# The fourth expert job in split form, its weights fetched early into staging buffers: a gated scan with a mixture of experts on Trainium2

## The chip, the cores and the metric

The kernel runs on one core of one Trainium2 chip. The metric is the device time of one execution in microseconds (us). An execution is repeated, and the median is quoted; one further execution is recorded by the hardware profiler.

## What is computed

The reference first runs a gated linear recurrence over 4 sequences of 3648 tokens with 256 features, and then sends every token to one of 16 experts.

```python
f = lower_bound + (1 - lower_bound) * sigmoid(f_logit)
for t in range(S):                       # per sequence
    h = f[:, t] * h + (1 - f[:, t]) * x[:, t]
    y[:, t] = h
# y is taken as 14592 rows of 256
g = argmax(y @ w_group)                  # one of 4 groups
e = argmax(y @ w_expert[g])              # one of 4 experts in it
out = softmax weights of g and e * (relu(y @ w1[g, e]) @ w2[g, e])   # 256 -> 1024 -> 256
```

All numbers are float32.

## The kernel before

**Units and jobs.** The tokens are cut into 29 units of 512 (28 full and one half). For each unit, phase 1 makes the gate, scans, writes the rows back in row form, computes the router's logits, and scatters each row to its expert's list in device memory. Of a group of units (one unit each for the first eight, then two) the routing is done together. The experts' work is cut into jobs. A job "A" takes the first rows of one expert's list as soon as enough units are scattered (its cut, the first number in `EARLY`); there are 16, and the first four take 256 rows each with cuts at units 4, 6, 8 and 8. A job "B" takes the rest of a list once all is scattered. Jobs are numbered from 0 here, as in the code: the fourth job is job 3.

**Two forms of a job.** A job with `j.raw` (line 865) multiplies in float32: its weights go by DMA straight into the weight tiles (line 959), `raw1` (line 1063, the matmuls at line 1071) makes the hidden layer, and `raw2` (line 1106, matmuls at line 1110) the output. ScalarE alone evicts the hidden layer (line 1074). A job in split form takes each float32 value as the sum of a float16 high part and a bfloat16 low part. Its weights land in a staging buffer `st` (line 963); `job_split` casts them on ScalarE (line 971) and subtracts on VectorE (line 973), four pieces to a job. The rows are cast at line 1042 and their low part is a subtraction at line 1043, with a small copy of the rows' numbers at line 1048. The first layer is three matmuls for each float32 one (lines 1097 to 1099), evicted by ScalarE (line 1102) and VectorE (line 1103) together; the second layer is line 1129.

**The order.** The main loop goes over the jobs. While it writes out job n it also writes out the preparation of job n+1 (`prep_thunks`: four times fetch and split, then the rows) and pieces of phase 1, paced by `due` marks. A raw job's second layer stands directly behind its first; that of a split job is left pending and stands behind the first layer of the next job. On SP (the queue that issues the loads) the written order is the executed one. On the other engines a planner of the framework reorders the main loop's instructions by its estimates.

**Fetching.** All weight pieces stand in one list, four to a job. `fetch_to(n)` issues loads until piece n; a job must have been chosen (`picked`) first. Job 0's pieces are fetched on its choosing, those of jobs 1 and 2 right behind job 0's row load (line 721). After that each preparation step fetches at most two pieces more, up to four ahead for a raw job and eight ahead for a split one (line 1215). There are 8 staging buffers, which units 4 to 7 of phase 1 use first for their inputs, and 3 buffers for each of the four weight tiles.

Of the kernel before, what the change touches and what calls it, by code (L numbers as in the profile page):

```python
# [22 lines left out]
EARLY = [(4, 2), (6, 2), (8, 2), (8, 2), (10, 2), (10, 2), (12, 3), (14, 3),  # L23
         (16, 4), (18, 4), (20, 4), (22, 5), (24, 5), (26, 5), (28, 5), (28, 5)]
# [8 lines left out]
ROWS_AT = {4: 5, 6: 7}  # L33
USED = float(1 << 22)
STG_BUFS = 8
RAW = 4
BOOK = 10
XR_BUFS = 6
ROW_BUFS = 6
# [14 lines left out]
def gated_scan_moe(ctx: ExitStack, tc, zx, lower, wroute, wexp, out, S):  # L54
# [391 lines left out]
    def p1_thunks(us, groups, parts):  # L446
# [54 lines left out]
        for u in us + [us[-1] + 1]:  # L501
            seq = []
            if u <= FAST:
# [39 lines left out]
                for m in [m for m, v in ROWS_AT.items() if u == v]:  # L543
                    f = lambda m=m: early_rows(m)
                    f.mark = m
                    put(f)
# [11 lines left out]
                if u == FAST:  # L558
                    f = lambda: None
                    f.mark = "begun"  # L560
                    put(f)
                    for v in [v for v in sorted(cuts) if v <= FAST and v not in ROWS_AT]:
                        f = lambda v=v: early_rows(v)
                        f.mark = v
                        put(f)
# [31 lines left out]
            if u - 1 in ends:  # L597
                grp = ends[u - 1]
                T = sum(unit_range(v)[1] - unit_range(v)[0] for v in grp) // P
                G = {}  # L600

                def bind(G=G, first=grp[0]):
                    G.update(cur.pop("G"))
                    G["rows"] = group_rows.pop(first)
                if u <= 13:
                    s1, f4x, s2, f3, f4, s6, f5, s7s = route_thunks(G, T, True)
                    rs = [s1, s2, f3, f4x, None, f4, s6, f5]
                else:
                    s1, s2, s3, s4, s5, s6, s7s = route_thunks(G, T)
                    rs = [s1, s2, s3, None, None, s4, s5, s6]  # L610
                rs.append(("scat", s7s))
                put(bind)
                rs.append(lambda u=u: choose(u))
                if u in cuts:
                    rs.append(lambda u=u: place(u))
                    f = lambda u=u: early_rows(u)
                    f.mark = u
                    rs.append(("lag", f))
                hold.extend(rs)
# [68 lines left out]
    def blanks():  # L688
        while unblanked:
            j = unblanked.pop(0)  # L690
            m = 1 if EARLY[j.idx][1] == 2 else 2
            sync.dma_start(out=xs_v[NT + j.idx][bass.ds(j.e * LW + (PRE - m * P), m * P), :].rearrange("(p k) c -> p k c", k=m),
                           in_=blank[:, None, :].broadcast_to([P, m, RW]))
# [20 lines left out]
    def early_rows(u):  # L714
        for mac in macros:
            for j in mac:
                if j.kind == "A" and EARLY[j.idx][0] == u and j.idx < NE - 1:
                    job_rows(j)
        ready[0] = True
        if u == EARLY[0][0]:  # L720
            fetch_to(pptr[0] + 8)

    regs = {}
    early_loads = []
# [115 lines left out]
    def make_job(kind, idx):  # L840
# [6 lines left out]
        while at < j.len:  # L847
# [16 lines left out]
            at += w  # L864
        j.raw = kind == "A" and idx < RAW
        j.wh, j.wl, j.st = {}, {}, {}
# [88 lines left out]
    def job_weights(j, i):  # L955
        e = job_e(j)
        if j.raw:
            w = wp.tile([P, 1024], F32, name=f"w{i}")
            sync.dma_start(out=w, in_=wexp[bass.ds(e * P, P), i * 1024:(i + 1) * 1024])
            j.wh[i], j.wl[i] = w[:, 0:512], w[:, 512:1024]  # L960
            return
        st = stg.tile([P, 1024], F32, name="st")
        sync.dma_start(out=st, in_=wexp[bass.ds(e * P, P), i * 1024:(i + 1) * 1024])
        j.st[i] = st
# [199 lines left out]
    pptr = [0]  # L1164
# [24 lines left out]
    def bg_to(n):  # L1189
        while done[0] < n:  # L1190
            bg_pop()

    def fetch_to(n):
        while pptr[0] < min(n, len(pieces)):
            j, i = pieces[pptr[0]]
            if j.kind == "A" and j.idx not in picked:
                return
            if j.kind != "A":
                bg_to(marks["order"])
            job_weights(j, i)  # L1200
            pptr[0] += 1
        if ready[0]:
            ready[0] = False
            blanks()
# [158 lines left out]
```

## Time and profile before

| | us |
|---|---|
| median of 3 runs | 761.43 |
| the three runs | 761.33, 761.43, 763.17 |
| the profiled execution | 761.96 |
| its span in the trace | 760.2 |
| TensorE (PE) busy in the span | 715.6 |
| VectorE (DVE) busy | 514.6 |
| ScalarE (ACT) busy | 445.9 |
| GpSimd (POOL) busy | 296.3 |

The trace records each instruction with its start, its duration, and the releaser of the idle time before it. PE's matmuls are pipelined, so the distance between the starts of neighbours is what one costs, and not the recorded duration of one. "PEld" is the loading of weights into PE. A view by stretches adds up the busy time of every engine between two times, and what is missing from the stretch is waiting.

### The profile page before, as it was taken

How to read it: one execution, taken by the hardware profiler on the slowest of the kernel's cores; microseconds unless marked ns; L12 is line 12 of the kernel's file. 1: busy time of each engine (PE TensorE's matmuls, PEld its weight loads, DVE VectorE, ACT ScalarE, POOL GpSimd, SP SyncE). 2: the span in 40 equal slices, each digit the busy share in tenths (PEclk: the TensorE clock that was granted, in tenths of full speed). 3: DMA queues.
4: the chain of work that ended last, by engine and by line, in shares of the span. 5: the costliest groups of instructions: out<-in, count | busy, mean ns of one | idle time of the engine just before them, and what ended most of it. 6: DMA issues, size and time to landing. Idle time of an engine off the chain costs nothing.

```text
span 760.2 us, 17863 instructions
## 1 busy us (share of the span) xinstructions
PE 715.6 (94%) x6471; PEld 588.0 (77%) x6471; DVE 514.6 (68%) x1086; ACT 445.9 (59%) x827; POOL 296.3 (39%) x314
## 2 busy tenths in 40 slices
PE   3569999998899999999999999999999999999995
PEld 1457888886788888888999676867778886777895
DVE  6899758999799976495556754644644645755660
ACT  6567767887577855454545644544544545655651
POOL 3656267668567764632222121312122121123232
PEclk9999999999999999999999999999999999999998
DMA  8978789989888873657994470617155345655520
GB/s 326 413 255 292 243 351 289 408 316 310 289 258 292 242 211 117 170 146 189 222 241 106 113 189 29 169 43 188 47 155 131 114 133 168 196 174 170 168 65 23
DMA packets 100410, 151.35 MB, mean 199 GB/s; under 512 B 60203, under 2 KB 70206, under 8 KB 97504
## 3 DMA queue, kind: packets, MB, share of 16 engines
q1 hardware_dynamic: 85792, 102.84, 46.1%
q0 software_dynamic: 11408, 30.02, 10.7%
q10 hardware_dynamic: 3120, 17.34, 6.7%
q8 instruction: 51, 0.84, 0.5%
q14 instruction: 39, 0.32, 0.1%
HBM read 112.49 MB, written 37.96 MB: 198 GB/s over the span
## 4 chain that ended last, share of the span: by engine, by line
PE 71%; DVE 11%; issue 8%; DMA 3%; POOL 3%; ACT 2%; another core or an unknown queue 1%; SPq 1%; POOLq 0%; DVEq 0%
PE ps_m L1129 28%; PE ps_m L1099 7%; PE ps_m L1097 7%; PE ps_m L1098 7%; PE ps_m L1110 4%; PE ps_m L1071 4%; PE ps_p L1097 3%; PE ps_p L1098 3%; PE ps_p L1099 3%; PE ps_p L284 3%; POOL out_dram L1143 3%; DVE h L256 2%; DVE w L973 1%; PE ps_p L303 1%; DVE hl L1103 1%
## 5 line engine op out<-in xcount | busy, mean ns | idle before, releaser
L1129 PE MATMUL ps_m<-w,hh 128*128 128x256 f16 (+5 forms) x1260 | 218.9, 268 | 1.3 <-issue 1.3
L1129 PE MATMUL ps_m<-w,hl 128*128 128x256 f16 (+4 forms) x740 | 188.5, 267 | 0.6 <-issue 0.6
L973 DVE TENSOR_TENSOR w<-st,w 128x1024 bf16<-128x1024 f32 x112 | 135.8, 1219 | 68.2 <-ACT w L971 66.7
L393 POOL DMA_INDIRECT xs<-rows,posi x114 | 138.2, 1212 | 87.6 <-ACT rows L288 25.6
L1143 POOL DMA_INDIRECT out_dram<-o,info x67 | 71.6, 1069 | 244.1 <-ACT o L1141 226.6
L1129 PE MATMUL ps_m<-w,rows 128*128 128x256 f16 (+5 forms) x880 | 133.8, 267 | 0.3 <-issue 0.3
L1129 PEld LDWEIGHTS <-hh 128*128 128x128 f16 (+7 forms) x1260 | 117.9, 101 | 15.6 <-issue 3.3
L971 ACT CAST w<-st 128x1024 f16<-128x1024 f32 x112 | 116.1, 1047 | 17.6 <-PE ps_m L1129 12.5
L1097 PE MATMUL ps_m<-xh,w 128*128 128x256 f16 (+9 forms) x494 | 120.4, 256 | 2.5 <-DVE hl L1103 2.4
L1099 PE MATMUL ps_m<-xh,w 128*128 128x256 f16 (+9 forms) x494 | 120.3, 256 | 0.8 <-issue 0.8
L1098 PE MATMUL ps_m<-xl,w 128*128 128x256 bf16 (+9 forms) x494 | 120.3, 256 | 0.0
L1103 DVE SCALAR_TENSOR_TENSOR hl<-ps_m,hh 128x512 bf16<-128x512 f32 (+7 forms) x107 | 71.1, 671 | 40.6 <-ACT hh L1102 24.7
L1098 PEld LDWEIGHTS <-w 128*128 128x128 f16 x800 | 78.3, 98 | 25.3 <-issue 3.7
L1097 PEld LDWEIGHTS <-w 128*128 128x128 f16 x800 | 78.3, 98 | 23.2 <-issue 1.6
L1099 PEld LDWEIGHTS <-w 128*128 128x128 bf16 x800 | 78.3, 98 | 22.8 <-issue 0.4
L1143 POOL DMA_INDIRECT out_dram<-o,meta x47 | 53.4, 1136 | 101.8 <-ACT o L1141 69.1
L1129 PEld LDWEIGHTS <-rows 128*128 128x128 f16 (+4 forms) x880 | 81.6, 101 | 10.0 <-issue 0.6
L1102 ACT ACTIVATE hh<-ps_m 128x512 f16<-128x512 f32 (+7 forms) x107 | 63.3, 594 | 37.1 <-PE ps_m L1099 32.1
L1141 ACT ACTIVATE o<-ps_m,info 128x256 f32<-128x256 f32 (+4 forms) x67 | 31.1, 463 | 91.5 <-PE ps_m L1129 75.8
L1129 PEld LDWEIGHTS <-hl 128*128 128x128 bf16 (+4 forms) x740 | 70.8, 101 | 9.1 <-issue 1.9
L256 DVE TENSOR_TENSOR_SCAN h<-zt,h 128x512 f32<-128x512 f32 (+3 forms) x48 | 56.6, 1191 | 0.5
L1103 DVE SCALAR_TENSOR_TENSOR hh<-ps_p,rows 128x512 bf16<-128x512 f32 (+7 forms) x30 | 17.6, 586 | 45.4 <-ACT rows L1102 45.3
(203 smaller groups left out, 1183.4 us busy)
## 6 DMA issues: line engine op xcount, KB each, us to landing
st<-in_wexp_dram SPq DMA_DIRECT2D x112, 512.0 KB
zt<-in_zx_dram ACTq DMA_DIRECT2D x16, 1024.0 KB
w<-in_wexp_dram SPq DMA_DIRECT2D x16, 512.0 KB
xs<-blank SPq DMA_DIRECT2D x26, 258.0 KB
zt<-in_zx_dram SPq DMA_DIRECT2D x6, 1024.0 KB
st<-in_zx_dram SPq DMA_DIRECT2D x8, 512.0 KB
xr<-xs SPq DMA_DIRECT2D x12, 258.0 KB
xr<-xs SPq DMA_DIRECT2D x16, 129.0 KB
```

The source lines that it names most:

```text
L256: sn = nc.vector.tensor_tensor_scan(out=h[:, k, c0 - a:c1 - a], data0=ff[:, k, c0 - a:c1 - a], data1=uu[:, k, c0 - a:c1 - a], initial=init ...
L393: sc = nc.gpsimd.indirect_dma_start(out=xs_v[G["t0"] + t][:, :], out_offset=bass.IndirectOffsetOnAxis(ap=R["posi"][:, t:t + 1], axis=0), i ...
L971: nc.scalar.copy(j.wh[i], j.st[i])
L973: nc.vector.tensor_tensor(out=j.wl[i], in0=j.st[i], in1=j.wh[i], op=ALU.subtract)
L1097: nc.tensor.matmul(po, w1_at(j.wh, k, c), xh[:, k], start=(k == 0), stop=False)
L1098: nc.tensor.matmul(po, w1_at(j.wh, k, c), xl[:, k], start=False, stop=False)
L1099: nc.tensor.matmul(po, w1_at(j.wl, k, c), xh[:, k], start=False, stop=(k == KD - 1))
L1102: eviction[0] = nc.scalar.activation(hi, pv, AF.Relu).ins
L1103: nc.vector.scalar_tensor_tensor(out=h_at(j.hl[ch], cs, slice(0, w)), in0=pv, scalar=0.0, in1=hi, op0=ALU.max, op1=ALU.subtract)
L1129: nc.tensor.matmul(pm[i * q:i * q + n, 0:dw], h_at(h[ch], [c], ts)[:, 0], w2_at(w, c)[:, i * dw:(i + 1) * dw], start=(c == 0 and s == 0), ...
L1141: nc.scalar.activation(o[s, 0:dw], pm[s, 0:dw], AF.Copy, scale=lt.bitcast(F32)[s, r, 1:2])
L1143: nc.gpsimd.indirect_dma_start(out=out_v[out_n[0]].rearrange("n (g d) -> (n g) d", g=g), out_offset=bass.IndirectOffsetOnAxis(ap=lt[s, r, ...
```

## The change

The constant `RAW`, the number of jobs that run in float32, goes from 4 to 3, so that job 3 is in split form: its weights go to staging buffers and are split there, and its second layer stands behind the first layer of job 4. And `early_rows`, which issues a job's row load, fetches four more pieces at unit 6's cut, right behind the row load of job 1; these are the pieces of job 3.

```diff
-RAW = 4
+RAW = 3
...
         ready[0] = True
-        if u == EARLY[0][0]:
-            fetch_to(pptr[0] + 8)
+        if u in (EARLY[0][0], EARLY[1][0]):
+            fetch_to(pptr[0] + (8 if u == EARLY[0][0] else 4))
```

## Rows read from the trace of the kernel before

**Rows 1.** The page's part 4: the chain that ended last, by engine.
```profile
PE 71%; DVE 11%; issue 8%; DMA 3%; POOL 3%; ACT 2%; another core or an unknown queue 1%; SPq 1%; POOLq 0%; DVEq 0%
```
**Rows 2.** Busy time by stretches: stretch, its length, busy us (instructions) by engine.
```profile
60.00:98.00 38.00, 37.77 (x279) 30.61 (x280) 30.39 (x78) 27.91 (x64) 17.36 (x19) 1.00 0.80 269
98.00:136.00 38.00, 38.00 (x241) 32.21 (x240) 27.14 (x63) 27.17 (x55) 26.11 (x31) 1.00 0.92 319
136.00:192.00 56.00, 52.42 (x568) 44.24 (x567) 55.57 (x110) 46.40 (x87) 39.83 (x37) 1.00 0.96 340
192.00:210.00 18.00, 15.54 (x151) 13.38 (x148) 12.48 (x30) 8.96 (x22) 10.35 (x12) 1.00 0.87 290
210.00:280.00 70.00, 68.84 (x687) 60.33 (x686) 67.78 (x141) 55.12 (x105) 51.26 (x52) 1.00 0.80 252
...
350.00:740.00 390.00, 389.26 (x3418) 310.86 (x3416) 223.06 (x377) 207.37 (x358) 85.09 (x79) 1.00 0.52 142
```
**Rows 3.** Timeline of PE, 120 to 140 us: start, duration, line, operation, count.
```profile
120.23 0.60 PE L1071 MATMUL ps_m<-xh,w 128*128 128x256 f32 x2
...
133.77 1.03 PE L1110 MATMUL ps_m<-w,hh 128*128 128x256 f32 x4
134.63 1.89 PE L1110 MATMUL ps_m<-w,hl 128*128 128x256 f32 x8
...
138.90 0.27 PE L1098 MATMUL ps_m<-xl,w 128*128 128x256 bf16 x1
...
139.99 0.27 PE L1099 MATMUL ps_m<-xh,w 128*128 128x256 f16 x1
```
**Rows 4.** The page's part 5, three groups of split jobs: busy, mean ns, idle.
```profile
L973 DVE TENSOR_TENSOR w<-st,w 128x1024 bf16<-128x1024 f32 x112 | 135.8, 1219 | 68.2 <-ACT w L971 66.7
...
L971 ACT CAST w<-st 128x1024 f16<-128x1024 f32 x112 | 116.1, 1047 | 17.6 <-PE ps_m L1129 12.5
...
L1103 DVE SCALAR_TENSOR_TENSOR hl<-ps_m,hh 128x512 bf16<-128x512 f32 (+7 forms) x107 | 71.1, 671 | 40.6 <-ACT hh L1102 24.7
```
**Rows 5.** Waits of DVE, 98 to 136 us: total us, times, longest.
```profile
DVE zt L245 <- ACT zt L229: 5.6, 4, 2.6
DVE sc L432 <- PE ps_p L421: 2.6, 1, 2.6
DVE mx L330 <- ACT Lg L317: 2.3, 2, 1.3
```
**Rows 6.** Timeline of DVE, 117 to 136 us, idle before in brackets.
```profile
117.57 2.34 DVE L973 TENSOR_TENSOR w<-st,w 128x1024 bf16<-128x1024 f32 x2
...
124.19 1.23 DVE L245 SCALAR_TENSOR_TENSOR zt<-zt 128x1024 f32<-128x1024 f32 x1 [0.61 <-ACT zt L229]
...
130.15 0.68 DVE L1043 TENSOR_TENSOR xl<-ps_p,xh 128x512 bf16<-128x512 f32 x1
130.75 0.32 DVE L1048 COPY meta<-xr 128x4 int32<-128x4 int32 x1
...
135.88 1.23 DVE L245 SCALAR_TENSOR_TENSOR zt<-zt 128x1024 f32<-128x1024 f32 x1 [1.07 <-ACT zt L229]
```
**Rows 7.** Timeline of SP's issuing, 72 to 117 us: start, duration, line, load, count.
```profile
72.41 0.36 SPq L692 DMA_DIRECT2D xs<-blank  x1
81.57 2.97 SPq L946 DMA_DIRECT2D xr<-xs  x4
...
88.10 6.54 SPq L959 DMA_DIRECT2D w<-in_wexp_dram  x4
...
113.14 3.33 SPq L946 DMA_DIRECT2D xr<-xs  x4
```
**Rows 8.** Timeline of POOL at 117 us.
```profile
117.63 2.36 POOL L711 TENSOR_TENSOR got<-got,sel 128x16 f32<-128x16 f32 x1
```
**Rows 9.** Line 711 on POOL: duration ns min/median/max, first and last start.
```profile
L711 POOL TENSOR_TENSOR got<-got,sel x10: 207/218/2362, 97.8 to 302.2; 128x16 f32<-128x16 f32 x10
```
**Rows 10.** The staging buffers' readers on DVE, 60 to 215 us, columns as in rows 9.
```profile
L973 DVE TENSOR_TENSOR w<-st,w x21: 1198/1217/1243, 117.6 to 212.2; 128x1024 bf16<-128x1024 f32 x21
```

## The prediction

> **What bounds the kernel now.** I read the chain of work that ended last first. PE holds most of it, and DVE is a distant second [rows 1]. That is an average over stages, so the next view is busy time by stretches [rows 2]. From 350 to 740 us PE works 389.26 of 390 us: whatever PE is given late in that stretch moves the end. Between 98 and 136 us PE has no gap at all, while DVE works 27.14 of 38 us and so waits 10.86. From 136 to 192 us it is the other way round: DVE works 55.57 of 56 us and PE waits 3.58. From 192 to 210 us both have some room (PE waits 2.46, DVE 5.52); from 210 to 280 us neither has (68.84 and 67.78 of 70). So PE is the bound of the long tail, and DVE is the bound just behind the place that is changed. Job 3 runs in the one stretch in which PE is full and DVE is not. PE's timeline shows its first matmul at 120.23 us and its last eight from 134.63 us [rows 3].
>
> **What PE gains.** In float32 a 256-wide product takes two instructions. Four of them lie between the starts at 133.77 and 134.63 us [rows 3], which is 0.86 / 4 = 0.215 us each. Job 3 has 8 blocks x 2 halves in the first layer and 2 row tiles x 8 blocks in the second, 32 products, so 64 x 0.215 = 13.76 us. In split form each product is three instructions. Ten starts lie between 138.90 and 139.99 us [rows 3], 0.109 us each: 96 x 0.109 = 10.46 us. PE gains 3.30 us, all of it in a stretch where it never waits, so it is on the path there.
>
> **What DVE and ACT pay.** DVE gets four subtractions of weights at 1.219 us, four evictions at 0.671 us [rows 4], one subtraction of the rows at 0.68 us and one copy at 0.32 us [rows 6]: 4.88 + 2.68 + 0.68 + 0.32 = 8.56 us. ACT gets four casts at 1.047 us, 4.19 us [rows 4]; its four evictions of the hidden layer remain, and one cast of the rows replaces two copies. ACT waits 38 - 27.17 = 10.83 us of the stretch [rows 2], and this hides its 4.19 us. I cost ACT at nothing; without that cover it would be those 4.19 us, and they would come out at DVE's gates, which wait for ACT (below).
>
> **Whether DVE can hide it.** Suppose PE kept its whole gain: the stretch from 98 us shrinks to 38 - 3.30 = 34.70 us, and DVE has 27.14 + 8.56 = 35.70 us to do in it. Even without a single wait it ends 1.00 us over, so the stretch becomes 35.70 us, plus whatever DVE still waits. The end then moves by 35.70 + w - 38 = w - 2.30 us, w being the waiting that stays. Three kinds of wait are there [rows 5]: 5.6 us for ACT in front of the gates, 2.6 us for PE's ranking matmuls, 2.3 us for the logits. The first preparation steps of a job are written out with the first layer of the job before it, so job 3's belong to the start of job 2, just after 98 us. There the listed waits, less the two late gates of 0.61 and 1.07 us [rows 6] and one wait for logits (2.3 - 1.3 = 1.0 us), are 10.5 - 2.68 = 7.8 us in four pieces, for 4.88 + 0.68 + 0.32 = 5.88 us of work. The 1.9 us left over there can take one of job 4's splits forward, whose weights come sooner (below). The evictions fall behind 120 us, where the three waits left hold 2.68 us for as much work. But the two late gates wait for ACT, which in turn runs behind PE; I see nothing that fills these, and take w = 0.61 + 1.07 = 1.68 us. Ends for w: 0, and all 10.86 us. The value is near the low end because the splits are short (1.2 us) against waits of up to 2.6 us, and depend on nothing late: their weights are fetched early. So the move is 1.68 - 2.30 = -0.62 us.
>
> **What comes behind.** A move of DVE at 136 us is carried through 56 us in which it never stops, and PE cannot use a lead there: it waits for DVE. From 210 us both are full again, and from 350 us PE is. Nothing later takes the move back or adds to it. The second layer of job 3 moves behind the first layer of job 4, which gives PE work in reserve for some 5 us, but job 4's rows and splits are wanted that much sooner, and these are DVE's. Its cost is not shown in the trace; the nearest row is PE's waiting from 136 to 192 us, 3.58 us [rows 2], which it could remove or double. I take nothing for it, since DVE's order of work sets that stretch, and keep both ends.
>
> **The fetch.** On SP the four early loads stand behind job 1's row load and ahead of the blank rows at 72.41 us; SP then issues nothing until 81.57 us [rows 7]. Four such loads took 6.54 us to issue at 88.10 us [rows 7], at most: 72.41 + 6.54 + 0.36 = 79.3 us, still ahead of the row loads of jobs 2 and 3. The staging buffers that they take are those of units 4 and 5, long read by then. So the fetch costs nothing; without that room the row loads would slip by up to 6.54 us, and PE has jobs 1 and 2 to do meanwhile. The four loads at 88.10 us go, and job 4's pieces move up to them. One wait is new: now job 5's first pieces are fetched in job 3's preparation and need its staging buffers, so SP stands until its splits are done. Behind it in SP's queue are blank rows and the row loads of jobs 4 and 5 (113.14 us [rows 7]), for which job 4's first layer waits. With the splits done by about 110 us that is hidden; each us past 113.14 would delay these rows by one, which PE would see only from the time when job 4's row split (130.15 us before [rows 6]) is late for it. Price: nothing; at worst, if the splits stood as late as those at 117.57 us [rows 6], some 117.57 + 2.34 - 113.14 = 6.8 us less room for the rows, and no more than that.
>
> **A rule that speaks against it.** POOL's small product at line 711 takes 0.218 us as a rule, but 2.36 us at 117.63 us, just as DVE does two splits (117.57 us, 2.34 us) [rows 6, 8, 9]. DVE's own splits vary only from 1.198 to 1.243 us in 21 cases [rows 10], so here POOL waits and not DVE. POOL works 26.11 of 38 us [rows 2]: four more splits can hold it for 4.88 us, in 11.89 us of room. The Trainium skill, "SBUF — State Buffer", section "Who interferes with whom", says that a DVE instruction with two inputs in SBUF contends with a GpSimd instruction that reads SBUF, and that whichever began first holds the other up entirely. By that rule DVE could be the one held; rows 8 show the other half of it, and rows 10 show no split that was held. As a mechanism of this kernel this is the third rival below, with a small chance.
>
> **The rivals.** *The whole gain.* The splits slide ahead of 98 us, into the 7.61 us that DVE waits from 60 to 98 us [rows 2]: with 1.00 + 1.68 us of work moved there, PE keeps 3.30 us, and the time is 761.43 - 3.30 = 758.1 us. For it: the weights land long before, and DVE's waits there are as many. Against: this asks the planner to hoist a step by more than one job. *DVE becomes the bound.* The gates' waits stay, since ACT has casts ahead of its own part of the gate: w = 5.6 us, a move of +3.3 us, 764.7 us. For it: these are the longest waits, and DVE already has no room behind 136 us. It decides from w over 2.30 us. *The port.* Each added split is held by a POOL instruction of about its own length, 4.88 us more for DVE: -0.62 + 4.88 = +4.3 us, 765.7 us. Rows 10 speak against it. *It doesn't do what it says.* The planner puts job 3's second layer and preparation where PE's order is as before, and its saving becomes waiting for DVE: 761.4 us.
>
> **How the numbers follow.** The profiled execution took 761.96 us, its span 760.2 and 1.76 outside it; the median is 761.43, or 0.53 less. The change of the span is taken off the median: 761.43 - 0.62 = 760.8 us. Chances: this forecast 0.40, the whole gain 0.32, DVE as the bound 0.21, the port 0.03, no effect 0.04. About 0.3%, or 2.3 us, is what a measurement here can tell from no change; so faster 0.32, same 0.44, slower 0.24. The range goes from a little under the whole gain (a third of the 3.58 us of PE's waiting removed too: 756.9) to past the two slower rivals, 765.8 us.
>
> **What would show it.** Right: DVE works 35 us or more of the stretch from 98 us, four more splits lie before 115 us, job 4's first matmul starts 0 to 2 us after job 3's first layer with no wait, and PE's waits up to 192 us grow by about 2.5 us. The whole gain: splits before 98 us, and no more waiting of PE. DVE as the bound: gates still waiting over a us each for ACT, and PE waiting over 7 us from 136 to 192 us. The forecast fails most simply if the planner's new order moves DVE's routing work past the splits, since that chain feeds everything behind.

## The result and the profile after

The changed kernel takes 770.82 us (median of 6 runs, 768.20 to 772.07), the kernel before 761.38 us beside it (759.72 to 764.18): 1.0117 times as long, 95% interval 1.0089 to 1.0145. The forecast was 760.8 us, the range ended at 765.8 us. The profiled execution after took 771.69 us, with a span of 769.9 us, 9.7 us more than before.

First, busy time by the stretches of [rows 2]; columns as there.

```profile
60.00:98.00 38.00, 34.09 (x249) 26.71 (x248) 28.13 (x73) 24.39 (x57) 14.40 (x13) 0.94 0.81 284
98.00:136.00 38.00, 36.65 (x260) 30.22 (x260) 28.67 (x57) 28.21 (x52) 25.31 (x28) 0.97 0.76 255
136.00:192.00 56.00, 51.37 (x515) 43.57 (x515) 53.31 (x116) 43.75 (x83) 35.38 (x34) 0.97 0.96 321
...
350.00:740.00 390.00, 389.15 (x3389) 309.84 (x3388) 223.58 (x386) 206.48 (x358) 83.19 (x78) 1.00 0.54 147
```

The tail from 350 us is as full as before. The loss begins ahead of 98 us, where the prediction had put a price on nothing: PE works 34.09 of 38 us there (37.77 before) and its mean granted clock is 0.94. In the two stretches behind, PE waits 1.35 and 4.63 us (nothing and 3.58 before) although it has less to do.

What came late is seen in SP's timeline, against [rows 7] (start, duration, line, load, count), and in SP's waits from 60 to 130 us (total, times, longest).

```profile
69.96 0.94 SPq L946 DMA_DIRECT2D xr<-xs  x2
71.32 2.73 SPq L963 DMA_DIRECT2D st<-in_wexp_dram  x4
82.91 0.35 SPq L692 DMA_DIRECT2D xs<-blank  x1
89.21 2.92 SPq L946 DMA_DIRECT2D xr<-xs  x4
95.74 0.91 SPq L692 DMA_DIRECT2D xs<-blank  x2
100.44 19.05 SPq L963 DMA_DIRECT2D st<-in_wexp_dram  x7
126.75 2.92 SPq L946 DMA_DIRECT2D xr<-xs  x4
```
```profile
SPq L963 <- DVE w L973: 12.8, 2, 10.4
...
SPq L692 <- DMA zt<-in_zx_dram: 8.6, 1, 8.6
```

The four early loads are issued in 2.73 us, well inside the room of the forecast. But the blank rows behind them go out at 82.91 us instead of 72.41: SP stands 8.6 us until a load of `zt` lands that the blank rows have nothing to do with. The row loads of jobs 2 and 3 slip from 81.57 to 89.21 us. The chain of waits of this stretch (start, duration, what) goes exactly there:

```profile
72.37 10.41 DMA zt<-in_zx_dram
...
82.91 6.16 DMA xs<-blank
...
89.77 5.07 DMA xr<-xs
```

Why that load: a completion semaphore is a counter that a load raises when it has landed. In the compiled program the loads of SP and ACT take eight of them in turn, and SP waits ahead of a load until the last user of its semaphore has landed. With four loads put in front, the blank rows get the semaphore whose last user is a 1 MB load that ACT issued at 72 us, and that wait stands in the program right ahead of them. PE's timeline shows what the lateness costs (idle time in brackets); the busy time by steps of 2 us beside it has the granted clock as the third number from the end, as a share of full speed.

```profile
92.08 0.36 PE L1033 MATMUL ps_p<-ident,xr 128*128 128x128 f32 x1 [1.02 <-DMA xr<-xs]
94.88 0.91 PE L1033 MATMUL ps_p<-ident,xr 128*128 128x128 f32 x3 [2.44 <-DMA xr<-xs]
```
```profile
90.00:92.00 2.00, 1.06 (x5) 0.58 (x4) 2.00 (x4) 1.54 (x5) 0.00 (x0) 1.00 0.84 238
92.00:94.00 2.00, 0.36 (x1) 0.20 (x1) 1.48 (x4) 0.00 (x0) 0.00 (x0) 0.89 0.96 393
94.00:96.00 2.00, 1.12 (x4) 0.79 (x5) 0.00 (x0) 0.17 (x1) 0.00 (x0) 0.50 0.49 166
...
98.00:100.00 2.00, 2.00 (x6) 1.55 (x6) 0.73 (x7) 0.84 (x2) 1.42 (x2) 0.50 0.10 37
```

After that pause the clock is granted at 0.50, the lower of its two levels (1.2 and 2.4 GHz), from 94 to 100 us.

### The profile page after: what moved, and what is told of

Read it like the earlier page. It is cut to its first block, busy times and chain, and to the rows that moved or that the text cites. A ratio compares the mean times of both kernels' runs of the same rounds, so it can differ in the third digit from the quotient of the medians.

```text
span 769.9 us, 17942 instructions
## 1 busy us (share of the span) xinstructions
PE 716.5 (93%) x6503; PEld 585.8 (76%) x6503; DVE 522.7 (68%) x1096; ACT 450.1 (58%) x830; POOL 295.1 (38%) x314
## 4 chain that ended last, share of the span: by engine, by line
PE 60%; DVE 12%; issue 11%; DMA 8%; POOL 4%; ACT 2%; SPq 1%; POOLq 0%; DVEq 0%; ACTq 0%
PE ps_m L1129 26%; PE ps_m L1097 6%; PE ps_m L1098 6%; PE ps_m L1099 6%; PE ps_p L1097 3%; PE ps_p L1099 3%; PE ps_p L1098 3%; POOL out_dram L1143 3%; DMA zt<-in_zx_dram 2%; DVE h L256 2%; DVE w L973 2%; PE ps_p L284 2%; PE ps_m L1071 2%; PE ps_m L1110 2%; DVE hl L1103 2%
## 5 line engine op out<-in xcount | busy, mean ns | idle before, releaser
L1129 PE MATMUL ps_m<-w,hh 128*128 128x256 f16 (+7 forms) x1292 | 224.7, 268 | 1.7 <-issue 1.4
L1129 PE MATMUL ps_m<-w,hl 128*128 128x256 f16 (+5 forms) x756 | 192.5, 267 | 0.3 <-issue 0.2
L973 DVE TENSOR_TENSOR w<-st,w 128x1024 bf16<-128x1024 f32 x116 | 140.6, 1219 | 73.4 <-ACT w L971 71.0
L1129 PEld LDWEIGHTS <-hh 128*128 128x128 f16 (+7 forms) x1292 | 120.8, 101 | 16.6 <-issue 4.1
L971 ACT CAST w<-st 128x1024 f16<-128x1024 f32 x116 | 120.0, 1047 | 18.2 <-PE ps_m L1129 13.9
L1097 PE MATMUL ps_m<-xh,w 128*128 128x256 f16 (+9 forms) x510 | 125.4, 258 | 4.2 <-DVE hl L1103 2.5
L1098 PE MATMUL ps_m<-xl,w 128*128 128x256 bf16 (+9 forms) x510 | 125.4, 258 | 1.6 <-issue 1.6
L1099 PE MATMUL ps_m<-xh,w 128*128 128x256 f16 (+9 forms) x510 | 125.4, 258 | 0.2 <-issue 0.2
L1103 DVE SCALAR_TENSOR_TENSOR hl<-ps_m,hh 128x512 bf16<-128x512 f32 (+7 forms) x111 | 73.9, 672 | 38.8 <-ACT hh L1102 26.6
L1098 PEld LDWEIGHTS <-w 128*128 128x128 f16 x816 | 80.2, 98 | 26.3 <-issue 4.3
L1097 PEld LDWEIGHTS <-w 128*128 128x128 f16 x816 | 80.0, 98 | 24.2 <-issue 2.4
L1129 PEld LDWEIGHTS <-hl 128*128 128x128 bf16 (+5 forms) x756 | 72.4, 101 | 8.5 <-issue 1.5
```

The source lines that it names most:

```text
L971: nc.scalar.copy(j.wh[i], j.st[i])
L973: nc.vector.tensor_tensor(out=j.wl[i], in0=j.st[i], in1=j.wh[i], op=ALU.subtract)
L1097: nc.tensor.matmul(po, w1_at(j.wh, k, c), xh[:, k], start=(k == 0), stop=False)
L1098: nc.tensor.matmul(po, w1_at(j.wh, k, c), xl[:, k], start=False, stop=False)
L1099: nc.tensor.matmul(po, w1_at(j.wl, k, c), xh[:, k], start=False, stop=(k == KD - 1))
L1103: nc.vector.scalar_tensor_tensor(out=h_at(j.hl[ch], cs, slice(0, w)), in0=pv, scalar=0.0, in1=hi, op0=ALU.max, op1=ALU.subtract)
```

## A ruler for the stretch: the gates

DVE runs one gate (line 245) per unit in phase 1, and each unit's gate waits for ACT, whose work waits for PE. So the starts of the gates show where a kernel falls behind. I name them by their times before: 88, 95, 114, 124, 136 and 161 us (88.04, 95.11, 113.59, 124.19, 135.88 and 161.40 us; those at 104.70 and 147.41 us between them are left out). The table, taken from DVE's timelines (the runs in it are described below), gives the time from one to the next in us; the last column is the growth from the first to the last over before, beside the growth of the time as measured (ratio with its interval; each against the kernel before on the same chip, whose medians were 759.75 to 761.87 us, and 751.98 us for e4, e6, e8 and e10).

| kernel | 88-95 | 95-114 | 114-124 | 124-136 | 136-161 | growth | time, ratio |
|---|---|---|---|---|---|---|---|
| before | 7.07 | 18.48 | 10.60 | 11.69 | 25.52 | | |
| after | 13.54 | 20.60 | 9.98 | 15.44 | 24.04 | 10.24 | 1.0117 [1.0089, 1.0145] |
| e1 split only | 7.07 | 20.60 | 9.97 | 15.31 | 24.07 | 3.66 | 1.0068 [1.0047, 1.0088] |
| e2 blank rows first | 7.07 | 20.60 | 9.97 | 16.44 | 24.06 | 4.78 | 1.0055 [1.0040, 1.0069] |
| e5 loads alone | 11.08 | 18.47 | 10.61 | 11.68 | 26.55 | 5.03 | 1.0044 [1.0029, 1.0059] |
| e6 split, fetched later | 7.07 | 20.61 | 10.00 | 16.86 | 24.05 | 5.23 | 1.0067 [1.0036, 1.0097] |
| e7 blank rows first, 5 ahead | 7.06 | 20.61 | 9.98 | 16.10 | 24.04 | 4.43 | 1.0095 [1.0065, 1.0125] |
| e10 low parts on ACT | 7.07 | 23.76 | 8.91 | 17.85 | 24.03 | 8.26 | 1.0107 [1.0073, 1.0141] |
| e11 no subtractions | 7.07 | 20.60 | 9.96 | 15.72 | 24.05 | 4.04 | 1.0086 [1.0052, 1.0119] |
| e12 three early loads | 7.07 | 20.61 | 10.01 | 15.22 | 24.05 | 3.60 | 1.0068 [1.0046, 1.0090] |
| e13 after again | 7.07 | 20.61 | 10.01 | 16.73 | 24.03 | 5.09 | 1.0140 [1.0106, 1.0175] |
| e15 order alone | 7.07 | 18.47 | 10.61 | 13.19 | 24.06 | 0.04 | 1.0010 [0.9991, 1.0028] |
| e16 no weight split | 7.07 | 18.41 | 10.43 | 14.54 | 24.05 | 1.14 | 1.0026 [1.0000, 1.0053] |
| e21 casts alone | 7.06 | 22.39 | 9.07 | 18.11 | 24.04 | 7.31 | 1.0123 [1.0097, 1.0149] |
| e24 casts behind a gate | 7.07 | 22.69 | 9.40 | 15.55 | 24.04 | 5.39 | 1.0073 [1.0054, 1.0092] |

Each row is one profiled execution. In every row but one the growth at the 161 us gate is within 2 us of what that execution took over the median of before, so what comes behind gives next to nothing back. The exception is e11, with 4.04 us at the gate and a profiled span 8.4 us longer than that of before: PE waits another 1.7 us from 210 to 280 us there (67.12 us busy, 68.84 before), and the rest I have not followed. The steps don't repeat equally well. That from 95 to 114 us is 20.60 or 20.61 us in every kernel with the change's four casts in the planner's own places. That from 124 to 136 us goes from 15.22 to 17.17 us in the same kernels (17.17 and 16.96 in e3 and e4, which the table leaves out), and after and e13, which are one kernel, have 15.44 and 16.73. So a difference of 1.3 us in that column, and in the growth, says nothing by itself.

## Experiments on the fetch

Three theories at first: A, the early loads are in the wrong place; B, DVE has too much to do; C, SP stands before the later rows because it waits for job 3's splits.

**The two halves of the change, and the order of the loads.** e1 is before with `RAW = 3` alone. e2 is after, with the blank rows issued ahead of the early loads:

```diff
         if u in (EARLY[0][0], EARLY[1][0]):
+            if u == EARLY[1][0]:
+                ready[0] = False
+                blanks()
             fetch_to(pptr[0] + (8 if u == EARLY[0][0] else 4))
```

> Job 3 in split form, without the early fetch: its pieces are fetched in its own preparation, behind the row loads of jobs 2 and 3, and the blank rows stand where they stood before. Theory A (the early loads push the blank rows, and with them the row loads of jobs 2 and 3, some 8 us later, and PE waits for these rows): no such delay, row loads of jobs 2 and 3 near 81.6 us, PE full from 90 to 100 us, time 759 to 763 us. Theory B (VectorE has no room for the split job): the loss stays, 767 us or more. Theory C (SP stands in front of the row loads of jobs 4 and 5 until job 3's splits free its staging buffers): here the same stand is left, so some 3 to 5 us of loss stay, 764 to 766 us.

> The changed kernel with one thing moved: at unit 6's cut the blank rows of job 3 are issued ahead of the four early loads instead of behind them. Same work, same loads. Theory A: the blank rows go out near 73 us instead of 82.9, the row loads of jobs 2 and 3 near 82 instead of 89.2, the wait of PE for these rows (3.5 us) is gone, and 6 to 9 us come back: 761 to 765 us. Theory B: no change from 770.8 us. Theory C: SP still stands before the row loads of jobs 4 and 5, so at most half comes back.

Measured: e1 765.10 us against 759.99, 1.0068; e2 763.92 us, 1.0055 [1.0040, 1.0069]. The change falls into two halves of about the same size: the split form costs 0.6 to 0.7%, the place of the early loads as much again, and reordering two lines takes the second away. In e2 the blank rows go out at 72.36 us and the row loads at 83.18 us, and PE has no wait for rows.

**Loads alone, three loads, after again.** e5 is before with four loads of 512 KB into staging buffers that nobody reads, ahead of the blank rows at unit 6's cut, and nothing else. e12 is after with three early loads (`4` becomes `3` in the diff of the change). e13 is after once more, beside it.

> The kernel before, with job 3 in float32 as it was, plus four loads of 512 KB into staging buffers behind job 1's row load, which nothing reads, and the blank rows behind them. Theory A: the loss comes from the place of these loads alone: blank rows after 80 us, row loads of jobs 2 and 3 near 89 us, time 766 to 771 us. Theory B and C: the loads by themselves cost nothing, 760 to 763 us (2 MB more traffic in a stretch where the DMA queues are 0.8 busy).

> The changed kernel with three pieces fetched early instead of four. The blank rows still stand behind the early loads, but by the round of eight semaphores that SP's and ScalarE's loads share they now have another one, whose last user landed long ago; with four pieces it is that of a 1 MB unit load. Theory A1 (what holds the blank rows is that semaphore): they go out within 2 to 4 us behind the early loads, near 75 us, PE's wait for the rows of job 2 is gone, and the time is that of e2, some 4 to 5 us below the changed kernel. Theory A2 (what holds them is the transfers ahead of them, three quarters of which are still there): they go out at 79 us or later, and at most 2 us come back.

> The changed kernel once more, beside the three that follow, on one chip: 1.0 to 1.4% slower than before, blank rows after 82 us and PE waiting about 3.5 us for the rows of job 2. It is the yardstick for them.

Measured: e5 763.18 us against 759.99, 1.0044 [1.0029, 1.0059]; its blank rows went out at 79.87 us, behind 8.9 us of waiting for the same `zt` load. So the loads cost by themselves, with no split in the kernel. e12 767.75 us against 761.87, 1.0068 [1.0046, 1.0090], e13 773.52 us, 1.0140 [1.0106, 1.0175]. One load fewer shifts the blank rows to a semaphore that is free: they go out at 74.13 us, SP no longer waits for `zt`, and half of the loss is gone. In the compiled program the wait for ACT's load no longer stands ahead of them. Since three loads are three quarters of the bytes, it is the turn of the semaphores, not the traffic, that does most of it. One thing stays open: in the profiled execution of e13, the quickest of its six (768.52 us), the blank rows were as late (83.28 us) and yet the gate of 95 us was on time. What PE sees is the row loads behind them. They went out at 89.21 us in after and 88.16 us in e3, where PE waited 3.5 and 3.8 us for rows, and at 87.39 us in e13 and 87.15 us in e12, where it waited for none. So the late rows hold PE in one profiled execution of this kernel and not in the other, and e12's rows, 5.6 us later than before, come early enough.

**SP in front of the later rows (theory C).** The prediction had named this wait: job 5's pieces stand for job 3's splits, with the row loads of jobs 4 and 5 behind. e3 is after with job 3's preparation fetching at most 4 pieces ahead; e6 is the same edit on e1, e4 on e2, and e7 is e2 with 5 pieces.

```diff
-            fetch_to(max(at + 1, min(at + (4 if j.raw else STG_BUFS), pptr[0] + 2)))
+            fetch_to(max(at + 1, min(at + (4 if j.raw or j.idx == 3 else STG_BUFS), pptr[0] + 2)))
```

> The changed kernel, but job 3's preparation fetches no more than four pieces ahead, as it did in float32, so that SP reaches the row loads of jobs 4 and 5 without standing for job 3's staging buffers. The blank rows stay behind the early loads. Theory A: the 3.5 us wait for the rows of jobs 2 and 3 stays and nearly all of the loss with it, 768 to 771 us. Theory B: no change. Theory C: the rows of jobs 4 and 5 come 8 us or more sooner than at 126.8 us and most of the loss is gone, 762 to 765 us.

> Job 3 in split form, no early fetch (as e1), and its preparation fetches at most four pieces ahead, so that SP does not stand for job 3's staging buffers in front of the row loads of jobs 4 and 5. Theory B (VectorE's added work, 8.6 us into 10.9 us of waits that it can't all use, moves everything behind): the loss of e1 stays, 763 to 766 us against 760.0. Theory C (the row loads of jobs 4 and 5, 119.7 us in e1 against 113.1): they come near 114 us and the loss is gone, 760 us or less.

> The changed kernel with both repairs: blank rows ahead of the early loads, and four pieces ahead in job 3's preparation. Theory B: what e2 left stays, 763 to 765 us. Theory C: back to 760 us or below it.

> Blank rows ahead of the early loads (e2), and in job 3's preparation at most five pieces ahead: all four of job 4's pieces are fetched ahead of the row loads of jobs 4 and 5, and none of job 5's, so that SP neither stands for job 3's staging buffers nor brings job 4's last piece late. Theory B (VectorE): 0.4 to 0.7% slower than before still. Theory C (SP's order): within 0.2% of before, or faster.

Measured: e3 770.74 us against 759.99, 1.0140 [1.0119, 1.0161]; e6 757.61 against 751.98, 1.0067; e4 759.41 against 751.98, 1.0102 [1.0072, 1.0132]; e7 769.56 against 761.87, 1.0095 [1.0065, 1.0125]. None is better than its base (e3 and e6 beside after and e1, e4 and e7 beside e2; each pair ran on two chips, so that only the ratios compare). The stand of SP is real (12.8 us in the waits of after, the row loads of job 4 at 126.75 instead of 113.14 us, of which some 10 us are the lateness of the whole kernel there), and these runs show no cost of it. The cure has a side effect: job 4's last piece comes late, ACT stands for it, and everything in ACT's order behind it is late, up to the eviction at 139.11 us that DVE and then PE wait for:

```profile
134.75 1.05 ACT L974 CAST w<-st 128x1024 f16<-128x1024 f32 x1 [3.75 <-DMA st<-in_wexp_dram]
...
140.12 0.37 PE L1100 MATMUL ps_m<-xh,w 128*128 128x256 f16 x1 [3.83 <-DVE hl L1106]
```

These lines are e4's. e6 has such a stand of 3.63 us too and is no slower than e1, so that it is what e4 pays is not shown.

Theory C falls, and theory A holds for half of the loss.

## Experiments on the split form

**DVE's work (theory B).** e11 is e7 with job 3's four subtractions of weights left out. e8 is before with eight subtractions of 512 columns from job 3's weights into a buffer that nobody reads. e10 is e6 with job 3's low parts made by a second cast on ACT.

> As e7, but the four subtractions of job 3's weights are left out (its matmuls with the low part take the high part again, so PE's work is the same; the result lacks the low part). VectorE loses 4.9 us of its added 8.6 us and nothing is put elsewhere. Theory B: 2.5 to 5 us faster than e7, at or below before. If VectorE's added work isn't what holds the stretch: within 1 us of e7.

> The kernel before, with job 3 in float32 and all its products unchanged, plus VectorE work alone in job 3's preparation: eight subtractions of 512 columns (about 0.65 us each, 5.2 us in all) from the weight tiles into a staging buffer that nothing reads. Theory B: VectorE has waits for part of it, and PE has not become faster, so 1 to 4 us slower than before. Theory C, or any theory in which VectorE's work is hidden in its 10.9 us of waits: 760 us.

> As e6, but job 3's low parts are written by ScalarE as a second cast of the weights instead of VectorE's subtraction (the part of the computation that is changed: the low parts then hold the whole weight and not the remainder). VectorE loses 4.9 us of its added 8.6, ScalarE gets 4.2 us more. Theory B: 2 to 4 us faster than e6. If VectorE isn't what sets the stretch: no faster than e6, or slower, as ScalarE's gates come later.

Measured: e11 770.15 us against 761.87, 1.0086, no better than e7. Busy time from 98 to 136 us, e1 first, then e7, then e11:

```profile
98.00:136.00 38.00, 36.70 (x280) 30.74 (x280) 30.85 (x58) 29.49 (x55) 25.02 (x27) 1.00 0.88 305
```
```profile
98.00:136.00 38.00, 35.70 (x272) 29.94 (x271) 29.97 (x56) 28.67 (x54) 24.91 (x28) 1.00 0.83 268
```
```profile
98.00:136.00 38.00, 36.45 (x272) 30.29 (x272) 25.93 (x52) 28.30 (x54) 25.81 (x28) 1.00 0.79 253
```

DVE has 4.04 us less to do in e11 than in e7 and simply waits that much longer; the gates stand where they stood. So the sum of DVE's work is not what binds, and theory B falls as far as the subtractions go; the evictions, which stay in e11, come up again below. e8 (760.76 against 751.98, 1.0115 [1.0087, 1.0143]) tells nothing on it: DVE, which works in order, stood for weights that landed late, and PE's loss came ahead of 98 us. e10 lost more, 759.55 us against 751.98, 1.0107 beside e6's 1.0067. It takes work from DVE and gives it to ACT, and was the first sign that ACT is the place.

**The order of the two layers.** e15 is before, job 3 still in float32, but with its second layer left behind job 4's first (in the main loop, `j.raw` becomes `j.raw and j.idx != 3` in the two places that decide it).

> The kernel before, job 3 in float32 as ever, but its second layer left behind job 4's first layer; nothing else is changed. If the order of the two layers by itself costs what is left of the split form (0.6 to 0.9%), this is 4 to 6 us slower than before, and the second and third base additions (line 381) start some 4 us later. If the order costs nothing, as the prediction had it, within 1.5 us of before.

Measured: 760.86 us against 760.03, 1.0010. In the table the 124-136 us step grows by 1.50 us and the next one shrinks by 1.46: the order moves work past a gate and back. It costs nothing, as forecast.

**The form on PE, without the splitting.** e16 loads job 3's weights as before and feeds the 16-bit high halves to PE as they are, three products for each; ACT's casts and DVE's subtractions of weights are gone, the evictions and the new order stay. e19 adds four idle casts on ACT to e16, e20 four idle subtractions on DVE.

> Split form on PE alone: job 3 runs three 16-bit products for each, with the evictions on DVE, the cast and the subtraction of the rows, and its second layer behind job 4's first; its weights are loaded as before, and their 16-bit high halves are used as they are, so the four casts on ACT and the four subtractions on DVE are left out (the values of this job are not the reference's). In PE's order the two ranking matmuls (lines 355 and 356) stand right behind job 3's first layer again, as before, and not behind 23 products of its second. If the splitting of the weights, on whichever engine, is what costs, this is 0 to 3.3 us faster than before (PE's gain, less 3.36 us of added DVE work that finds room or not). If it is the form on PE, the evictions or the order of the layers, it is slower than before by 4 to 6 us as e1 was.

> e16 with four casts of 1024 columns on ACT at the places of job 3's casts, from the identity matrix into a staging buffer that nobody reads. If ACT's casts stand in front of its part of the gates and so make everything behind later (in e1 the second gate behind 104 us started at about 116.3 us instead of 113.6), this is 2 to 4 us slower than e16, and the gate at 113.6 us comes 2 to 3 us later. If ACT's room hides them, as the prediction had it, within 1 us of e16.

> e16 with four subtractions of 1024 columns on DVE at the places of job 3's, of the identity matrix from itself into a staging buffer that nobody reads. If the sum of DVE's work is what costs, up to 4.9 us slower than e16. If DVE has room between 98 and 136 us, as e11 says, within 1 us of e16.

Measured: e16 762.05 us against 760.03, 1.0026; e19 761.47 us, 1.0020 [0.9997, 1.0043]; e20 770.96 us, 1.0140 [1.0105, 1.0176]. So without any splitting of weights the form is still no gain: at the 161 us gate it is 1.14 us behind, all from the step 124-136 us, where the evictions and the row split are new on DVE (e19 has 1.01 us). e19 and e20 miss their purpose. With nothing to wait for, the planner slid the idle work ahead, the casts to 42 to 50 us and the subtractions to 39 to 44 us. There the casts are free, while DVE's four stand in the middle of the routing chain. DVE's timeline of e20 has the first of them, and PE's the ranking matmul that waited:

```profile
39.22 1.23 DVE L974 TENSOR_TENSOR st<-ident 128x1024 bf16<-128x1024 f32 x1
```
```profile
49.56 0.21 PE L419 MATMUL ps_p<-oh16f,upto 128*128 128x64 bf16 x1 [7.12 <-DVE oh16f L407]
```

In e16 that matmul waited 3.23 us. The 4.96 us of work cost 9 us over e16, because of where they stood. What they cost behind 98 us these two don't say.

**ACT's casts in their places.** e21 is e16 with the same four casts, each held behind a ReLU of job 2, which brings them to 104 to 110 us. e24 is the real e1 with its four casts held behind ACT's part of the gate at 104.70 us.

```diff
-        nc.scalar.copy(j.wh[i], j.st[i])
+        with tc.issue_after(affine[14]) if j.kind == "A" and j.idx == 3 else ExitStack():
+            nc.scalar.copy(j.wh[i], j.st[i])
```

> e16 with four casts of 1024 columns on ACT, of the identity matrix into a staging buffer that nobody reads, each held behind the ReLU of job 2's first layer that is written out before it, which puts them at the places of job 3's own casts between 104 and 111 us (in e19 nothing held them and they slid ahead to 40 to 60 us). The four subtractions stay left out, and job 3's values are not the reference's. With the casts there, PE's order has the two ranking matmuls behind 23 products of job 3's second layer again, as in e1; in e16 they stand right behind its first. If the casts in their places are the cost, 2 to 4 us slower than e16 and as far from before as e1 (0.6 to 0.8%). If ACT's room hides them, within 1 us of e16 (0.1 to 0.4% over before).

> e1 with job 3's four casts on ACT held behind ACT's part of the gate at 104 us, which they partly stood ahead of in e1 (the cast at 103.56 us, the gate's lines 229 at 104.49 us); nothing else is changed, and the splits still lie before 120 us. If casts ahead of the gates are the cost, the gate of 113.6 us in before comes back from 116.3 us to about 114 us, and the time to within 0.3% of before. If the cost is elsewhere, 0.6 to 0.8% over before as in e1.

Measured: e21 768.03 us against 759.75, 1.0123, some 6 us more over its before than e16; e24 765.88 us, 1.0073, no better than e1. The two gates between which the casts lie, in before, e1, e11, e16 and e21:

```profile
95.11 1.23 DVE L245 SCALAR_TENSOR_TENSOR zt<-zt 128x1024 f32<-128x1024 f32 x1 [1.62 <-ACT zt L229]
...
113.59 1.23 DVE L245 SCALAR_TENSOR_TENSOR zt<-zt 128x1024 f32<-128x1024 f32 x1 [1.30 <-ACT zt L229]
```
```profile
95.66 1.23 DVE L245 SCALAR_TENSOR_TENSOR zt<-zt 128x1024 f32<-128x1024 f32 x1 [1.62 <-issue]
...
116.26 1.22 DVE L245 SCALAR_TENSOR_TENSOR zt<-zt 128x1024 f32<-128x1024 f32 x1 [0.51 <-ACT zt L229]
```
```profile
96.72 1.23 DVE L245 SCALAR_TENSOR_TENSOR zt<-zt 128x1024 f32<-128x1024 f32 x1 [1.62 <-issue]
...
117.32 1.23 DVE L245 SCALAR_TENSOR_TENSOR zt<-zt 128x1024 f32<-128x1024 f32 x1 [1.16 <-issue]
```
```profile
95.93 1.23 DVE L245 SCALAR_TENSOR_TENSOR zt<-zt 128x1024 f32<-128x1024 f32 x1 [1.61 <-issue]
...
114.34 1.23 DVE L245 SCALAR_TENSOR_TENSOR zt<-zt 128x1024 f32<-128x1024 f32 x1 [0.47 <-ACT zt L229]
```
```profile
94.04 1.23 DVE L245 SCALAR_TENSOR_TENSOR zt<-zt 128x1024 f32<-128x1024 f32 x1 [1.62 <-issue]
...
116.43 1.23 DVE L245 SCALAR_TENSOR_TENSOR zt<-zt 128x1024 f32<-128x1024 f32 x1 [1.16 <-ACT zt L229]
```

18.41 to 18.48 us without casts of job 3 in between (before, e15, e16), 20.60 or 20.61 with its four (after, e1, e6, e11), whether or not DVE subtracts behind them, and 23.76 with eight (e10). ACT's timeline shows where they stand, before and in e1:

```profile
103.15 1.52 ACT L229 ACTIVATE zt<-zt,mid,half 128x512 f32<-128x512 f32 x2
...
110.55 1.06 ACT L219 ACTIVATE zt<-zt 128x1024 f32<-128x1024 f32 x1
...
112.02 1.53 ACT L229 ACTIVATE zt<-zt,mid,half 128x512 f32<-128x512 f32 x2
```
```profile
103.56 1.03 ACT L971 CAST w<-st 128x1024 f16<-128x1024 f32 x1
104.49 1.52 ACT L229 ACTIVATE zt<-zt,mid,half 128x512 f32<-128x512 f32 x2
...
106.39 1.04 ACT L971 CAST w<-st 128x1024 f16<-128x1024 f32 x1
...
108.77 2.01 ACT L971 CAST w<-st 128x1024 f16<-128x1024 f32 x2
...
112.72 0.58 ACT L1042 CAST xh<-ps_p 128x512 f16<-128x512 f32 x1 [0.84 <-PE ps_p L1033]
113.21 1.06 ACT L219 ACTIVATE zt<-zt 128x1024 f32<-128x1024 f32 x1
114.69 1.53 ACT L229 ACTIVATE zt<-zt,mid,half 128x512 f32<-128x512 f32 x2
```

The next gate's part on ACT (lines 219 and 229) starts at 110.55 us before and at 113.21 us in e1, behind the casts. e24 moves all four casts behind the first gate, and the second pays for all four: 22.69 us. ACT's busy time between the gates of 95 and 114 us (the fourth of the busy times), before, in e1 and in e24, is the account:

```profile
95.11:113.59 18.48, 18.48 (x142) 15.32 (x142) 10.46 (x23) 11.20 (x26) 11.96 (x16) 1.00 0.87 351
```
```profile
95.66:116.26 20.60, 20.60 (x140) 17.57 (x140) 16.34 (x35) 15.27 (x31) 13.89 (x16) 1.00 0.99 377
```
```profile
95.23:117.92 22.69, 22.23 (x146) 18.66 (x145) 15.57 (x29) 15.43 (x31) 12.16 (x15) 1.00 0.95 372
```

ACT was idle 7.28 us of this step before, 5.33 us in e1 and 7.26 us in e24: of 4.07 and 4.23 us of added work, its idle time took up 1.95 us in e1 and next to nothing in e24. So the casts cost 2.1 to 4.2 us at the gates, by where they stand among them; this much is shown. How much of it is their own time and how much the order that the planner makes around them was not separated: in e1 it puts the cast of job 3's rows (line 1042), with a wait of 0.84 us for PE, ahead of the gate's part, while in e16, without casts, line 219 comes first.

A late gate is not yet lost time of PE. From 98 to 126 us PE waits 0.02 us at most before and in e16, e1 and e21; the price falls behind. From 126 to 165 us, before, e16, e1 and e21:

```profile
126.00:165.00 39.00, 38.52 (x365) 34.07 (x364) 37.59 (x76) 33.02 (x62) 24.11 (x24) 1.00 0.97 351
```
```profile
126.00:165.00 39.00, 35.47 (x365) 29.98 (x364) 37.44 (x78) 31.43 (x58) 23.07 (x24) 1.00 0.99 356
```
```profile
126.00:165.00 39.00, 34.66 (x339) 29.08 (x339) 36.80 (x77) 29.37 (x52) 20.79 (x22) 0.96 0.93 329
```
```profile
126.00:165.00 39.00, 32.78 (x295) 26.05 (x293) 33.96 (x67) 25.70 (x47) 20.60 (x20) 0.91 0.98 343
```

PE waits 0.48, 3.53, 4.34 and 6.22 us there. Of these it waits 0.5, 2.5, 2.6 and 4.0 us for DVE's evictions of the hidden layer (line 1103 before). So without any casts, in e16, waits that are mostly for the evictions already use up the 3.30 us that PE gains; the casts add to the waits, and with them the granted clock falls to 0.96 and 0.91 on the mean.

What the casts do further on is only partly settled: e21 loses another 6.4 us in the step 124-136, where ACT stood 3.4 us for a late piece of weights, and there the planner put the two ranking matmuls behind 23 products of job 3's second layer. It does so in every kernel with the casts in place (e1, e7, e21, e24) and not in before, e15, e16, e19 or e20. What that place alone costs was not tried, nor were the evictions put back on ACT alone.

## Why the prediction was wrong, point by point

- **What bounds the kernel**: held. The tail is full in all kernels (389.15 us after, 389.24 us in e1), and the stretch to 192 us set the end.
- **What PE gains**: the size held, the use did not. In split form a product's instruction takes 0.109 us in e1 too, and the gain turned into waiting: from 98 to 192 us PE waits 6.16 us in e1, where [rows 2] have 3.58 us, and all that is added lies behind 126 us.
- **What DVE and ACT pay**: the step that failed for the split form. ACT's 4.19 us were costed at nothing under a cover of 10.83 us of waiting in 38 us. That was the wrong span to count over. Between the start of ACT's gate part at 102.07 us and the gate at 113.59 us ACT's idle time before was 0.34, 1.09 and 1.30 us, 2.73 us in all; four casts don't fit, and the step between the gates grew by 2.12 us. The prediction had even said where they would come out, "at DVE's gates". DVE's evictions were put into waits behind 120 us; in e16, with no weight split, PE waits 2.5 us for them from 126 to 165 us, where before it waited 0.5 us. So the form would have gained nothing even with the casts free (e16, 1.0026).
- **Whether DVE can hide it**: the sum w - 2.30 is only bookkeeping. With w = 38 - 30.85 = 7.15 us in e1 it gives +4.85 us beside 5.11 us measured, but that is partly luck, as the 38 us no longer hold the same work. By the gates of 95 and 136 us, DVE works 29.53 of 40.77 us before and 38.69 of 45.88 us in e1: 9.16 us more work, and 4.05 us less waiting. And w was taken as 1.68 us. The waits were treated as room that short DVE work fills. They are set by ACT and PE, and e11 shows that taking the DVE work out leaves the waits in place of it.
- **What comes behind**: nothing for the order of the layers was right (e15). "Nothing later takes the move back" held from 161 us on; between 136 and 161 us it is 1.5 us shorter in every kernel with the new order, which is that order's own shift coming back.
- **The fetch costs nothing**: the step that failed for the other half. The issue room was right and beside the point; the blank rows waited 8.6 us for a stranger's load, 6.47 us at the next gate in the profiled execution of after and nothing there in that of e13, about 0.45 to 0.85% of the time (e2 and e3 on one chip, 1.0055 and 1.0140; e7 and e13 on another, 1.0095 and 1.0140). Only the issue times on SP had been read, not what each issue waits for. The wait that was priced, SP's stand for job 3's splits, came as described, and e3 and e6 show no cost of it.
- **The rivals**: "DVE becomes the bound", 764.7 us by ACT's casts ahead of the gates, has the reason that the runs show for part of the loss, and nearly the time of e1 (765.10 us). It was given 0.21. But its signs did not come: in e1 DVE waits 0.7 us in all for ACT at the gates from 98 to 136 us (5.6 us before) and not over a us each, and PE waits 4.86 us from 136 to 192 us and not over 7; so the nearness of its time is partly luck. No rival held a cost of the early loads, so the sum of both lay outside the range.
- **The port**: no split was held. The Trainium skill ("SBUF — State Buffer", "Who interferes with whom") would have let a POOL instruction hold a DVE one entirely; the splits in after still take 1.22 us on the mean, as in [rows 10], from the same view by lines, 60 to 230 us:

```profile
L973 DVE TENSOR_TENSOR w<-st,w 128x1024 bf16<-128x1024 f32 x27 | 32.2, 1220 | 4.5 <-ACT w L971 4.5
```

No kernel here beats the one before; e15 equals it (1.0010).

## What to carry to other kernels

Work on a side engine is hidden only if it fits into that engine's idle time between two links of the chain it serves; idle time summed over a long stretch says little, since most of it is waiting for that same chain. Before moving a load ahead in a queue, ask not only how long it takes to issue but which completion the next transfers in that queue will wait for. A marker that recurs in the chain, here the gate of each unit, shows where a change loses its time while whole times scatter by several us; how well each step repeats has to be looked at first (here within 0.01 us from 95 to 114 us, and 1.3 us apart in two executions of one kernel from 124 to 136 us).

## What was not expected of the hardware

- A transfer can stand for another engine's transfer: the blank rows on SP waited 8.6 us for ACT's 1 MB load, because in the compiled program both use the same completion semaphore in turn. One load more or fewer in front decides it (e12: 74.13 us, after: 82.91 us).
- Short waits of PE can cost twice: after 3.46 us of waiting for rows within 5 us, the granted clock in after was 0.50 (1.2 GHz of 2.4) from 94 to 100 us, and a float32 product of line 1071 (two instructions) took 0.85 us there instead of 0.43.
- In e1, e2, e7, e11, e12 and e13 PE stood 1.1 to 2.6 us between 126 and 131 us for nothing that the trace shows ("issue"), and in after and e3 1.4 and 2.4 us between 132 and 137 us. e6, e10, e16 and e24 have no such stand there. Whether this belongs to the form or to the execution stays open.
